# Experts' matmul operands at another distance in SBUF, a pad tile dropped, and casts placed later

## The chip, the cores and the metric

One core of a Trainium2 chip. The metric is the device time of one execution in microseconds (us); the time shown is the median of three runs.

## The reference, cut to what matters

```python
X = rfft(x, axis=1)                      # x: 8 sequences of 2496 rows, 256 columns
Yr = shrink(Xr @ w_r - Xi @ w_i + b_r)   # soft threshold, lam = 0.01
Yi = shrink(Xr @ w_i + Xi @ w_r + b_i)
x = irfft(Yr + 1j * Yi, n=2496, axis=1).reshape(19968, 256)
logits = x @ w_gate + modality_bias[modality_id]
e_idx = argmax(logits); gate_w = softmax(logits)[e_idx]
for e in range(8):                       # each row goes to one expert
    h = maximum(x[mask] @ w1[e], 0.0)    # 256 -> 1024
    out[mask] = gate_w[mask, None] * (h @ w2[e])   # 1024 -> 256
```

## The kernel before

The first part (up to 596 us in the profile) makes the Fourier transforms, the mixing and the routing: every row gets a place in a sorted array `xs` in DRAM, with 256 more rows of room behind each expert's own. The second part, class `Experts` (L801 on), works through that array.

`Experts.run` (L1233) goes through 38 tiles of 512 rows and 2 of 256, one expert per tile, and five small tiles of at most 32 rows in between (`tiny`, L1166), which fill single steps of TensorE's order. A tile's weights stand in one of two sets of SBUF tiles, `wb[i % 2]`; a set is `w0`, `w1` (layer 1, columns split in two groups) and `w2`, `w3` (layer 2, rows split likewise). Set 0 lies in the pool `mw0` on the right side of SBUF, at the end of memory; set 1 lies in `mw1` on the left side, behind the other pools of the part.

All experts' matmuls are fp32r, 128 rows by 256 columns, with every value split into a high and a low part, so a product of two blocks is three matmuls (high by high, high by low, low by high):

- Layer 1 (`layer1`, L1008, matmuls at L1024): the moving operand is the rows, `xh{j}` and `xl{j}` of pool `mxs`; the stationary one a block of `w0` or `w1`. From tile 8 on the 2x2 block product is done with seven products instead of eight, from sums of weights (made once, `weight_sums`) and of rows (`sums`): 7 products of 6 matmuls for each column group, 84 for a tile. Tiles 0 to 7 take 8 products for each group, 96.
- ScalarE and VectorE make `hh` and `hl` (pools `mh0`, `mh1`) of layer 1's result.
- Layer 2 (`layer2`, L1082, matmuls at L1095): here `hh`, `hl` are the stationary operand and `w2`, `w3` the moving one; 16 groups of 6 matmuls, 96 for a tile.

TensorE's order is written out by hand. A tile has two phases, `grp` 0 and 1. In phase 0 of tile i layer 1 of its own second column group goes with layer 2 of its first one (weights `w1`, `w2` of set i % 2); in phase 1 layer 1 of tile i + 1, first group (`w0` of the other set), goes with layer 2 of tile i, second group (`w3` of set i % 2). The string of `order` says which comes at each of 15 steps: "121212121221212", where a 1 is one product of layer 1 (6 matmuls) and a 2 is 6 matmuls of layer 2.

Beside it, tables say at which step a piece of other work is issued: `FILL[0]` (L1219) for phase 0, `FILL[1]` for phase 1. "x" is one turn of `parts(i + 1)` (L938): ScalarE casts one block of the next tile's rows to `xh{j}` (L958) and GpSimd subtracts to `xl{j}` (L959), j in the order 0, 1, 3, 2, 4, 5, 6. Each `xh{j}` has one buffer, so the cast of the next tile waits until layer 1's product on the old block is done. Blocks 2 to 5 are the row sums, made in place in the tile `xt`. "o", "t" and "p" are the output, the sums and the transposes.

`setup_pads` (L612) fills a tile with zeros and a number out of range; `pads` (L618) and `fence` (L640) write it behind each expert's rows with DMAs of SyncE's queue. The generator `late` (L1584) routes the last sequence, then calls `pads` and `fence`; it moves on at seven steps of each phase (`LATE`).

The pools lie one behind the other in SBUF in the order of `pools` (L811): `mx`, `mtr`, `mc`, a filler `mq0`, `mxs`, `ms`, a hidden-layer pair `mh0` and `mh1`, a filler `mq1`, `mw1`, `mb`. Fillers are sized by `PADS` (L46) in columns of 4 bytes. Sizes in bytes per partition: an `xh` or `xl` tile 1024, `ms` three tiles of 2048, `hh` and `hl` 8192 each, `w0` and `w1` 14336, `w2` and `w3` 8192. All of these are multiples of 512, and so is every block that a matmul takes of them; what an operand's start is modulo 512 is therefore set by the fillers and by the tiles of `mc` alone.

```python
PADS = (56, 16)                                                             # L46
pad = lambda name, n: n and pool(name, 1).tile([128, n], F32, name=name + "t")
for u in range(2):                                                          # L1021
    for k, (lo, x) in enumerate(((0, xh), (0, xl), (1, xh))):
        nc.tensor.matmul(ps[:, u, :], w1[:, lo, u, blk, :], x, ...)         # stationary, moving
...
nc.tensor.matmul(ps, h[:, q, o], w2[:, lo, q, :], ...)                      # L1095
```

Of the kernel before, what the change touches and what calls it, by code (L numbers as in the profile page):

```python
# [9 lines left out]
F32 = mybir.dt.float32  # L10
F32R = mybir.dt.float32r
# [12 lines left out]
D = 256  # L24
# [7 lines left out]
GC = D + E  # L32
# [10 lines left out]
MORE = 16  # L43
NPL = 8
EARLY = (6 * SEQ - 8 * (TP - 1)) // TP + 1 - E
PADS = (56, 16)  # L46
W1 = 2 * 2 * 4 * 128
W2 = 2 * 4 * 256
RAW = (2, 4, 6, 8, 10)
# [107 lines left out]
class Attn:  # L157
# [5 lines left out]
    def pools(self, ctx, first):  # L163
        tc, nb = self.tc, self.nb
        pool = lambda name, bufs, **k: ctx.enter_context(tc.tile_pool(name=name, bufs=bufs, **k))

        self.w6, self.w3, self.wx = (first.enter_context(tc.tile_pool(name=name, bufs=bufs, side="right"))
                                     for name, bufs in (("w6", 5), ("w3", 4), ("wx", 4)))
        self.ww = pool("ww", 2)
        self.wo = {"wh": pool("wh", 2), "wl": pool("wl", 2)}  # L170
        self.cp = pool("consts", 1)
        self.w4 = pool("w4", 4)
        self.wX = pool("wX", 3)
        self.w2 = pool("w2", 2)
        self.w1 = pool("w1", 1)
        self.cl = pool("cl", 1)
        self.ps = pool("ps", 2, space=PSUM)
        self.dr = pool("dr", 3, space=DRAM)
        self.scr = [None] * nb
        self.xt, self.xs, self.parts = {}, {}, []  # L180
# [616 lines left out]
class Experts:  # L797
# [8 lines left out]

    def sets(self, ctx, i, **k):
        p = ctx.enter_context(self.tc.tile_pool(name=f"mw{i}", bufs=1, reuse_waits="tile", **k))
        return [p.tile([128, 2, 2, 7, 128] if n < 2 else [128, 2, 4, D], F32R, name=f"w{n}_{i}") for n in range(4)]

    def pools(self, ctx):  # L811
        nc, tc, rt = self.nc, self.tc, self.rt
        pool = lambda name, bufs, **k: ctx.enter_context(
            tc.tile_pool(name=name, bufs=bufs, reuse_waits="tile", **k))
        pad = lambda name, n: n and pool(name, 1).tile([128, n], F32, name=name + "t")
        self.x = pool("mx", 2)
        self.tr = pool("mtr", 1)
        self.cp = pool("mc", 1)
        self.ident = self.cp.tile([128, 128], F32, name="mident")
        nc.gpsimd.memset(self.ident, 0.0)  # L820
        nc.gpsimd.affine_select(out=self.ident, in_=self.ident, compare_op=ALU.not_equal, fill=1.0, base=0,
                                pattern=[[-1, 128]], channel_multiplier=1)
        pad("mq0", PADS[0])
        self.xp = pool("mxs", 1)
        self.s = pool("ms", 1)
        self.h = [pool("mh0", 1), pool("mh1", 1)]
        pad("mq1", PADS[1])
        self.wb.append(self.sets(ctx, 1))
        self.b = pool("mb", 2)
        room = rt.at.x1f[0]  # L830
        self.raw = (room[:, :2 * F].rearrange("p (c f) -> p c f", c=2),
                    room[:, 2 * F:2 * F + 8 * D].rearrange("p (c d) -> p c d", d=D))
        self.small, o = {}, 2 * F + 8 * D
        for nm, n in (("xt", GC), ("xc", 256), ("x", 256), ("hs", 256), ("h", 256), ("y", 256), ("ix", 1)):
            self.small[nm], o = room[:, o:o + n], o + n
        self.ps = pool("mps", 2, space=PSUM)
        self.hps = pool("mhps", 1, space=PSUM)
# [369 lines left out]
    def sort_half(self, i):  # L1207
# [9 lines left out]
    FILL1 = {0: "x", 1: "o", 4: "x", 7: "x", 13: "x"}  # L1217
    FILL2 = {0: "x", 1: "o", 3: "t", 4: "x", 6: "x", 9: "x", 10: "x", 14: "x", 15: "x"}
    FILL = (  # L1219
        {0: "x", 1: "o", 3: "t", 4: "x", 6: "xx", 8: "x", 11: "x", 13: "x"},  # L1220
        {1: "o", 3: "p", 5: "p"})
    LATE = (2, 3, 5, 7, 9, 10, 12)

# [9 lines left out]
    def run(self, late, *tail):  # L1233
# [4 lines left out]
        for i in range(NPL - 2, -1, -1):  # L1238
            t = self.tags[i + 1]
            self.tags[i] = [t[3]] + [j for j in range(7) if j not in t]  # L1240
        pieces = self.weight_sums()
        for i in range(2):
            self.load_x(i)
        self.rt.setup_pads(self.cp.tile([128, GC], F32, name="pad2"))
        self.rt.grid2 = self.rt.load_grid(self.cp, "c_grid2", 5 * E + 3)
        for n in range(4):
            self.load_w(1, n)
# [111 lines left out]
def build(tc, I, out, nb):  # L1359
    nc = tc.nc  # L1360
    with ExitStack() as outer:
# [3 lines left out]
        with ExitStack() as ctx:  # L1365
            at = Attn(tc, I, nb)
            rt = Route(outer, tc, I, at, nb)
            front = ExitStack()
            at.pools(ctx, front)
            ex = None  # L1370
# [42 lines left out]
            i = at.table_load("m", 0, nc.gpsimd)  # L1413
# [41 lines left out]
            for b in range(nb):  # L1455
                done = b == nb - 1
                for p in range(10):
                    i = 10 * b + p
# [50 lines left out]
                    if done and p == 8:  # L1509
                        front.close()  # L1510
                        assert not (sw.todo or sw.raw)
                        ex = Experts(outer, tc, I, out, rt, wsp, wss)
# [67 lines left out]
        with ExitStack() as ctx:  # L1580
            ctx.enter_context(tc.manual_schedule(engines={ET.PE, ET.Activation, ET.DVE, ET.Pool}))
            ex.pools(ctx)

            def late():  # L1584
                for state in chain(routing, rt.tiles_last(ex.cp)):
                    yield
                    if state == "pe":
                        for _ in range(3):
                            yield
                while rt.pending:  # L1590
                    rt.scatter(1)
                    yield
                    yield
                for _ in range(12):
                    yield
                rt.pads()
                for _ in range(8):
                    yield
                rt.fence()
                rt.late = True  # L1600


            ex.run(late(), *tail)
# [24 lines left out]
```

## Time and profile before

| | |
|---|---|
| median of 3 runs | 1458.16 us (1457.96 to 1460.24) |
| the profiled execution | 1462.81 us |
| its span, first to last instruction | 1460.9 us |
| TensorE busy | 98% |
| mean granted clock of TensorE | 0.992 |

An engine's busy time is the union of its instructions' spans. A matmul's record (some 279 ns) is longer than the distance to the next matmul's start (some 116 ns), because matmuls are pipelined; what a stream of matmuls takes is read from the starts.

### The profile page before, as it was taken

What the parts mean: (1) busy time and instruction counts of PE and PEld (TensorE: products, weight loads), DVE (VectorE), ACT (ScalarE), POOL (GpSimd) and SP (SyncE); (2) the same over time, 40 slices, a digit from 0 to 9 for tenths busy, and PEclk for the clock granted to TensorE, in tenths of its full rate; (3) what the DMA queues carried; (4) which work ended last, traced back from release to release, by engine and by line L of the source; (5) the groups of instructions that cost most, each with busy time, mean ns of one, the idle gap of its engine ahead of it and who ended that gap; (6) DMA issues with size and microseconds to landing.
All of it is one profiled execution on the core that took longest, in us unless ns stands there. A gap on an engine that the chain in (4) does not pass through costs nothing. (4 is left out here: it accounts for less than half of the span.)

```text
span 1460.9 us, 33883 instructions
## 1 busy us (share of the span) xinstructions
PE 1427.8 (98%) x12084; PEld 1366.1 (94%) x12084; DVE 900.3 (62%) x1721; ACT 782.0 (54%) x1675; POOL 793.0 (54%) x907
## 2 busy tenths in 40 slices
PE   8899999999999999999999999999999999999996
PEld 5889999998989999999999999999999999999995
DVE  4567575757575876667565665666566656665651
ACT  3465656565656454544445555555555555555542
POOL 2355767676767666366667543444344444444432
PEclk9999999999999999999999999999999999999998
DMA  8979686969696759687787288124122942682192
GB/s 265 264 236 297 212 284 214 298 215 299 200 297 182 224 180 290 198 248 249 240 277 245 70 291 268 38 59 115 32 60 58 338 126 59 203 261 59 44 355 80
DMA packets 245299, 289.82 MB, mean 198 GB/s; under 512 B 121232, under 2 KB 176267, under 8 KB 241925
## 3 DMA queue, kind: packets, MB, share of 16 engines
q1 hardware_dynamic: 225587, 244.64, 54.4%
q0 software_dynamic: 19408, 42.83, 9.3%
q8 instruction: 98, 1.61, 0.5%
q14 instruction: 76, 0.62, 0.1%
q10 hardware_dynamic: 130, 0.12, 0.0%
HBM read 322.80 MB, written 117.56 MB: 301 GB/s over the span
## 5 line engine op out<-in xcount | busy, mean ns | idle before, releaser
L1095 PE MATMUL y<-w,hh 128*128 128x256 f32 x2496 | 461.4, 279 | 0.0
L1095 PEld LDWEIGHTS y<-w,hh 128*128 128x128 f32 x2496 | 380.8, 189 | 3.7 <-issue 3.7
L1095 PE MATMUL y<-w,hl 128*128 128x256 f32 x1248 | 346.8, 278 | 1.1 <-DVE hl L1030 0.9
L1024 PE MATMUL X<-xh,w 128*128 128x256 f32 x1248 | 270.3, 281 | 0.0
L1128 POOL DMA_INDIRECT out<-o,ix x156 | 155.4, 996 | 182.4 <-ACT o L1112 145.7
L1095 PEld LDWEIGHTS y<-w,hl 128*128 128x128 f32 x1248 | 234.2, 188 | 1.7 <-DVE hl L1030 1.7
L1024 PEld LDWEIGHTS X<-xh,w 128*128 128x128 f32 x1248 | 212.6, 188 | 2.0 <-ACT hh L1029 1.6
L1024 PE MATMUL X<-xl,w 128*128 128x256 f32 x624 | 174.6, 280 | 0.6 <-POOL xl L959 0.6
L1030 DVE SCALAR_TENSOR_TENSOR hl<-Y,hh 128x512 fp32r<-128x512 f32 x140 | 96.8, 692 | 102.9 <-ACT hh L1029 102.8
L1029 ACT ACTIVATE hh<-Y 128x512 fp32r<-128x512 f32 x140 | 83.8, 599 | 119.0 <-DVE Y L1033 101.1
L959 POOL TENSOR_TENSOR xl<-tr,xh 128x256 fp32r<-128x256 f32 x94 | 70.4, 749 | 129.2 <-ACT xh L958 128.7
L1024 PE MATMUL Z<-xh,w 128*128 128x256 f32 x608 | 131.8, 281 | 0.7 <-DVE Y L1033 0.7
L382 PE MATMUL mx<-wmix,Xh 128*128 128x256 f32 x640 | 116.6, 305 | 7.5 <-DVE mx L372 7.2
L959 POOL TENSOR_TENSOR xl<-xt,xh 128x256 fp32r<-128x256 f32 x122 | 89.5, 746 | 58.5 <-ACT xh L958 57.2
L1024 PEld LDWEIGHTS X<-xl,w 128*128 128x128 f32 x624 | 117.1, 188 | 1.0 <-POOL xl L959 0.8
L1038 ACT COPY v<-X 128x512 f32<-128x512 f32 x180 | 105.6, 587 | 17.5 <-PE X L1024 10.3
L598 POOL DMA_INDIRECT xs<-x1b,si x88 | 90.0, 1023 | 41.5 <-DVE pl L430 19.6
L424 PE MATMUL pv<-pv,z 128*120 128x136 f32 x704 | 108.5, 279 | 1.0 <-ACT z L414 0.9
L598 POOL DMA_INDIRECT xs<-x,si x88 | 89.5, 1017 | 36.0 <-issue 16.7
L292 POOL TENSOR_TENSOR x1l<-x,x1h 117x512 fp32r<-117x512 f32 x59 | 75.6, 1284 | 60.8 <-ACT x1h L290 21.9
L382 PEld LDWEIGHTS mx<-wmix,Xh 128*128 128x128 f32 x640 | 92.4, 190 | 16.4 <-ACT x1h L290 3.6
L1024 PEld LDWEIGHTS Z<-xh,w 128*128 128x128 f32 x608 | 103.7, 188 | 0.9 <-DVE Y L1033 0.9
(261 smaller groups left out, 3435.8 us busy)
## 6 DMA issues: line engine op xcount, KB each, us to landing
w<-wsp SPq DMA_DIRECT2D x96, 1024.0 KB
w<-wss SPq DMA_DIRECT2D x64, 1024.0 KB
w<-wsp SPq DMA_DIRECT2D x64, 768.0 KB
a<-scr SPq DMA_DIRECT2D x160, 128.0 KB
x<-in_x SPq DMA_DIRECT2D x38, 512.0 KB
xt<-xs SPq DMA_DIRECT2D x152, 128.0 KB
scr<-ev SPq DMA_DIRECT2D x35, 480.0 KB
wsp<-wh SPq DMA_DIRECT2D x64, 256.0 KB
```

Source lines behind the costliest of these rows:

```text
L292: (nc.gpsimd if pool else nc.vector).tensor_sub(xl, x, xh)
L382: nc.tensor.matmul(mx[:, i, :], t[:, c, 1 - i, :], self.w[:, i, c, lo, :], start=False, stop=n == 5, skip_group_check=True)
L424: nc.tensor.matmul(ps[:PK, c * 128:c * 128 + D // 2 + E], self.z[:, o:o + 3, :, :].rearrange("p n k r -> p (n k r)"), self.pv[:, c, :], st ...
L598: i = self.nc.gpsimd.indirect_dma_start(out=self.xs, out_offset=bass.IndirectOffsetOnAxis(ap=si[:, k:k + 1], axis=0), in_=rows, in_offset= ...
L959: (nc.gpsimd if i or j in (0, 1, 6) else nc.vector).tensor_sub(sq(xl), v, sq(xh))
L1024: nc.tensor.matmul(ps[:, u, :], w1[:, lo, u, blk, :], x, start=start and u == k == 0, stop=k == 2, skip_group_check=True)
L1029: nc.scalar.activation(hh[:, par::2, o], v, AF.Relu)
L1030: nc.vector.scalar_tensor_tensor(hl[:, par::2, o], v, 0.0, hh[:, par::2, o], ALU.max, ALU.subtract)
L1038: nc.scalar.copy(v, ps)
L1095: nc.tensor.matmul(ps, h[:, q, o], w2[:, lo, q, :], start=grp == s % 2 == q == k == 0, stop=grp == 1 and q == 3 and k == 2, skip_group_che ...
L1128: ins = self.nc.gpsimd.indirect_dma_start(out=self.out, out_offset=bass.IndirectOffsetOnAxis(ap=ix, axis=0), in_=o, in_offset=None, bounds ...
```

## The change

It does four things.

1. **Addresses.** A filler of 16 columns (64 bytes) stands between `ms` and `mh0`, one of 112 columns (448 bytes) in front of `mw1`, and each weight set now holds `w2`, `w3`, 16 columns of filler, then `w0`, `w1`.
2. **The pad tile.** `pad2` (264 columns, 1056 bytes) is no longer in `mc`; the pad rows are filled into the small tile's buffer `small["xt"]`, a piece of the first part's tile `x1`.
3. **When the pad rows are filled.** `setup_pads` is called one turn of `late` ahead of `pads`, no longer at the start of the part.
4. **Casts.** `FILL[0]` has its third to seventh "x" at steps 7, 8, 10, 12 and 14 instead of 6, 6, 8, 11 and 13. `FILL1` and `FILL2`, which tiles 0 to 7 use, stay.

```diff
--- before.py
+++ after.py
@@ -43,7 +43,7 @@
 MORE = 16
 NPL = 8
 EARLY = (6 * SEQ - 8 * (TP - 1)) // TP + 1 - E
-PADS = (56, 16)
+PADS = (56, 16, 112)
 W1 = 2 * 2 * 4 * 128
 W2 = 2 * 4 * 256
 RAW = (2, 4, 6, 8, 10)
@@ -806,7 +806,9 @@
 
     def sets(self, ctx, i, **k):
         p = ctx.enter_context(self.tc.tile_pool(name=f"mw{i}", bufs=1, reuse_waits="tile", **k))
-        return [p.tile([128, 2, 2, 7, 128] if n < 2 else [128, 2, 4, D], F32R, name=f"w{n}_{i}") for n in range(4)]
+        w2 = [p.tile([128, 2, 4, D], F32R, name=f"w{n}_{i}") for n in (2, 3)]
+        p.tile([128, 16], F32, name=f"mq2_{i}")
+        return [p.tile([128, 2, 2, 7, 128], F32R, name=f"w{n}_{i}") for n in (0, 1)] + w2
 
     def pools(self, ctx):
         nc, tc, rt = self.nc, self.tc, self.rt
@@ -823,8 +825,9 @@
         pad("mq0", PADS[0])
         self.xp = pool("mxs", 1)
         self.s = pool("ms", 1)
+        pad("mq1", PADS[1])
         self.h = [pool("mh0", 1), pool("mh1", 1)]
-        pad("mq1", PADS[1])
+        pad("mq3", PADS[2])
         self.wb.append(self.sets(ctx, 1))
         self.b = pool("mb", 2)
         room = rt.at.x1f[0]
@@ -1217,7 +1220,7 @@
     FILL1 = {0: "x", 1: "o", 4: "x", 7: "x", 13: "x"}
     FILL2 = {0: "x", 1: "o", 3: "t", 4: "x", 6: "x", 9: "x", 10: "x", 14: "x", 15: "x"}
     FILL = (
-        {0: "x", 1: "o", 3: "t", 4: "x", 6: "xx", 8: "x", 11: "x", 13: "x"},
+        {0: "x", 1: "o", 3: "t", 4: "x", 7: "x", 8: "x", 10: "x", 12: "x", 14: "x"},
         {1: "o", 3: "p", 5: "p"})
     LATE = (2, 3, 5, 7, 9, 10, 12)
 
@@ -1241,7 +1244,6 @@
         pieces = self.weight_sums()
         for i in range(2):
             self.load_x(i)
-        self.rt.setup_pads(self.cp.tile([128, GC], F32, name="pad2"))
         self.rt.grid2 = self.rt.load_grid(self.cp, "c_grid2", 5 * E + 3)
         for n in range(4):
             self.load_w(1, n)
@@ -1591,8 +1593,10 @@
                     rt.scatter(1)
                     yield
                     yield
-                for _ in range(12):
+                for _ in range(11):
                     yield
+                rt.setup_pads(ex.small["xt"])
+                yield
                 rt.pads()
                 for _ in range(8):
                     yield
```

Start addresses of the operands in the built programs, bytes modulo 512 (all blocks of one kind share the value):

| operand | before | changed |
|---|---|---|
| `xh`, `xl` (moving, layer 1) | 416 | 384 |
| `hh`, `hl` (stationary, layer 2) | 416 | 448 |
| `w0`, `w1` of set 1 (stationary, layer 1) | 480 | 448 |
| `w0`, `w1` of set 0 | 480 | 480 |
| `w2`, `w3` of set 1 (moving, layer 2) | 480 | 384 |
| `w2`, `w3` of set 0 | 480 | 416 |

The left side's values follow from the sizes: the 1056 bytes of `pad2` are 2 x 512 + 32, so `xh` moves from 416 to 384. Set 0 hangs on the end of memory and doesn't move along.

Where the order of instructions changes, on ScalarE, in phase 0 of tile 11 (any tile from 8 on reads alike; `xh{j}_12` is block j of the next tile, `v2`, `v3` are layer 1's copies out of PSUM, `hh1_11` the hidden layer). Before:

```order
L1038 COPY v2_11_1_12149<-X_11_1_12093 128x512
L958 CAST xh1_12_12151<-tr_12_11946 128x256
L958 CAST xh3_12_12168<-xt_12_11739 128x256
L958 CAST xh2_12_12172<-xt_12_11739 128x256
L1038 COPY v3_11_1_12188<-X_11_1_12093 128x512
L1029 ACTIVATE hh1_11_12091<-Y_11_1_12094 128x2x256
L958 CAST xh4_12_12193<-xt_12_11739 128x256
L1029 ACTIVATE hh1_11_12091<-X_11_1_12093 128x2x256
L958 CAST xh5_12_12218<-xt_12_11739 128x256
L1029 ACTIVATE hh1_11_12091<-Z_11_1_12095 128x2x256
L958 CAST xh6_12_12237<-tr_12_11946 128x256
```

With the change:

```order
L1041 COPY v2_11_1_12154<-X_11_1_12098 128x512
L961 CAST xh1_12_12156<-tr_12_11951 128x256
L961 CAST xh3_12_12179<-xt_12_11742 128x256
L1041 COPY v3_11_1_12189<-X_11_1_12098 128x512
L1032 ACTIVATE hh1_11_12096<-Y_11_1_12099 128x2x256
L961 CAST xh2_12_12194<-xt_12_11742 128x256
L961 CAST xh4_12_12211<-xt_12_11742 128x256
L1032 ACTIVATE hh1_11_12096<-X_11_1_12098 128x2x256
L961 CAST xh5_12_12229<-xt_12_11742 128x256
L1032 ACTIVATE hh1_11_12096<-Z_11_1_12100 128x2x256
L961 CAST xh6_12_12248<-tr_12_11951 128x256
```

The cast of `xh2` has moved behind the copy `v3` and the activation of `Y`; the others stand behind the same instructions as before.

On GpSimd, where the experts' part begins (`mident` is an identity matrix, the DMAs are the routing's). Before:

```order
L820 MEMSET mident_8216 128x128
L821 AFFINE_SELECT mident_8216<-mident_8216 128x128
L614 MEMSET pad2_8277 128x264
L598 DMA xs_68<-x1b_112,si_6_0_7592 162304x264 x2
L615 MEMSET pad2_8277 128x1
```

With the change:

```order
L822 MEMSET mident_8217 128x128
L823 AFFINE_SELECT mident_8217<-mident_8217 128x128
L598 DMA xs_68<-x1b_112,si_6_0_7592 162304x264 x2
L916 CAST ix_0_8300<-g_0_8267 128x4
L513 TENSOR_TENSOR b0_7_7990<-omid_7_7988,mb_515 117x176
```

The two fills of `pad2` are gone from here.

On GpSimd again, between phases 0 and 1 of tile 11 (`xl6_11` is the last subtraction of the next tile's rows). Before:

```order
L959 TENSOR_TENSOR xl4_11_11856<-xt_11_11421,xh4_11_11855 128x256
L959 TENSOR_TENSOR xl5_11_11881<-xt_11_11421,xh5_11_11880 128x256
L959 TENSOR_TENSOR xl6_11_11900<-tr_11_11640,xh6_11_11899 128x256
L1128 DMA out_0<-o_10_1_12009,ix_10_11415 19968x256 x2
L913 CAST ix_12_12070<-g_12_11740 128x4
```

With the change:

```order
L962 TENSOR_TENSOR xl5_11_11890<-xt_11_11424,xh5_11_11889 128x256
L962 TENSOR_TENSOR xl6_11_11909<-tr_11_11643,xh6_11_11908 128x256
L614 MEMSET x1_67 128x264
L615 MEMSET x1_67 128x1
L1131 DMA out_0<-o_10_1_12014,ix_10_11418 19968x256 x2
L916 CAST ix_12_12075<-g_12_11743 128x4
```

The two fills of the pad rows, now in a piece of `x1`, stand between the last subtraction and the output's DMAs. TensorE's and VectorE's orders are the same as before, and so is SyncE's apart from the tile that the pad DMAs read.

## Rows read from the trace of the kernel before

**Rows 1.** The page, head and part 1: busy us (share), instructions.

```profile
span 1460.9 us, 33883 instructions
...
PE 1427.8 (98%) x12084; PEld 1366.1 (94%) x12084; DVE 900.3 (62%) x1721; ACT 782.0 (54%) x1675; POOL 793.0 (54%) x907
```

**Rows 2.** Windows, layer 1's matmuls (L1024): stretch, us, PE, PEld, clock, DMA share, GB/s.

```profile
596.00:1450.00 854.00, 488.77 (x3384) 434.91 (x3384) 1.00 0.56 169
```

**Rows 3.** The same stretch, layer 2's matmuls (L1095).

```profile
596.00:1450.00 854.00, 527.62 (x3744) 475.79 (x3744) 1.00 0.56 169
```

**Rows 4.** Waits of TensorE, 596 to 1450 us: total us, times, longest.

```profile
PE y L1095 <- DVE hl L1030: 0.9, 1, 0.9
PE Z L1024 <- DVE Y L1033: 0.7, 1, 0.7
PE X L1024 <- POOL xl L959: 0.6, 1, 0.6
```

**Rows 5.** Timeline of TensorE, tile 12, groups' first matmuls: start us, us, ..., count merged.

```profile
855.03 0.28 PE L1024 MATMUL X<-xh,w 128*128 128x256 f32 x1
...
855.72 0.39 PE L1095 MATMUL y<-w,hh 128*128 128x256 f32 x2
...
856.40 0.28 PE L1024 MATMUL Y<-xh,w 128*128 128x256 f32 x1
...
857.11 0.40 PE L1095 MATMUL y<-w,hh 128*128 128x256 f32 x2
...
857.82 0.28 PE L1024 MATMUL X<-xh,w 128*128 128x256 f32 x1
...
858.51 0.39 PE L1095 MATMUL y<-w,hh 128*128 128x256 f32 x2
...
875.97 0.28 PE L1024 MATMUL X<-xh,w 128*128 128x256 f32 x1
```

**Rows 6.** The same timeline, tile 0, layer 1 alone: matmuls 6 and 49.

```profile
597.00 0.39 PE L1024 MATMUL X<-xh,w 128*128 128x256 f32 x2
...
601.87 0.28 PE L1024 MATMUL X<-xh,w 128*128 128x256 f32 x1
```

**Rows 7.** The same timeline, the last run of layer 2 alone, 16 matmuls.

```profile
1446.30 0.28 PE L1095 MATMUL y<-w,hl 128*128 128x256 f32 x1
...
1448.07 0.28 PE L1095 MATMUL y<-w,hl 128*128 128x256 f32 x1
```

**Rows 8.** The same timeline, layer 1 behind the transposes of a small tile.

```profile
1040.90 0.38 PE L1024 MATMUL X<-xh,w 128*128 128x256 f32 x1
...
1041.71 0.39 PE L1095 MATMUL y<-w,hh 128*128 128x256 f32 x2
...
1042.39 0.28 PE L1024 MATMUL Z<-xh,w 128*128 128x256 f32 x1
...
1440.87 0.36 PE L1024 MATMUL Y<-xh,w 128*128 128x256 f32 x1
...
1441.07 0.28 PE L1024 MATMUL Y<-xl,w 128*128 128x256 f32 x1
...
1442.37 0.28 PE L1024 MATMUL Y<-xh,w 128*128 128x256 f32 x1
```

**Rows 9.** Windows of all engines over one tile: us, PE, PEld, DVE, ACT, POOL, ...

```profile
1093.90:1114.80 20.90, 20.90 (x182) 20.90 (x181) 13.01 (x21) 11.72 (x25) 9.27 (x13) 1.00 0.24 51
```

**Rows 10.** Groups by line, 771 to 1416 us: casts and subtractions, busy us, mean ns.

```profile
L958 ACT CAST xh<-xt 128x256 fp32r<-128x256 f32 x118 | 45.0, 404 | 39.5 <-POOL xl L959 35.5 <-issue 4.0
...
L959 POOL TENSOR_TENSOR xl<-xt,xh 128x256 fp32r<-128x256 f32 x118 | 86.6, 745 | 58.5 <-ACT xh L958 57.2
```

**Rows 11.** Timeline of GpSimd: the fills of the pad rows, and around 838 us.

```profile
582.67 0.31 POOL L614 MEMSET pad<- 128x264 f32 x1
...
585.58 0.13 POOL L615 MEMSET pad<- 128x1 f32 x1
...
835.55 0.74 POOL L959 TENSOR_TENSOR xl<-tr,xh 128x256 fp32r<-128x256 f32 x1 [1.23 <-ACT xh L958]
...
840.63 1.00 POOL L1128 DMA_INDIRECT out<-o,ix  x1 [4.34 <-ACT o L1112]
```

## The prediction

> **What bounds the kernel now.** I read the page first: TensorE is busy 98% of a span of 1460.9 us [rows 1]. Then the windows of the experts' part: 3384 matmuls of layer 1 and 3744 of layer 2, 7128 together, in 854 us [rows 2, 3]. In that stretch TensorE waits for other engines 0.9 + 0.7 + 0.6 = 2.2 us in all [rows 4], and the granted clock is 1.00, the 2.4 GHz level. So the part lasts as long as its matmuls take from start to start, and only a change of that pace can move the time by much. The window over one tile shows the matmul and the weight load side by side without a gap: 20.90 us busy each, of 20.90 [rows 9].
>
> The timeline then shows that the pace isn't one number. From layer 1's first matmul of tile 12 at 855.03 to that of tile 13 at 875.97 are 180 matmuls in 20.94 us, **116.3 ns** each. But inside, two paces take turns [rows 5]: the group of 6 at 855.03 takes 0.69 us and the next one 0.68 (fast); those at 856.40 and 857.11 take 0.71 each (slow); the one at 857.82 takes 0.69 (fast again). The pace changes where layer 2 hands over to layer 1 (856.40, 857.82), not where layer 1 hands over to layer 2 (855.72, 857.11, 858.51). Away from handovers each pace holds: 43 matmuls of layer 1 alone at the part's start take 601.87 - 597.00 = 4.87 us, **113.3 ns** each [rows 6]; 15 matmuls of layer 2 alone at the end take 1.77 us, **118.0 ns** each [rows 7]. Same shape, same clock; what differs between the layers is where their operands lie. By the table of addresses layer 1's moving operand starts 64 bytes below its stationary one (416 and 480 modulo 512), layer 2's 64 bytes above. At a handover both ends swap, so the distance goes from one sign to the other.
>
> **The change, part by part.** The sum is made on the profiled execution, 1462.81 us, of which 1.9 lie outside the span; the median is 1458.16, 0.3% less, and I subtract the same microseconds from it.
>
> *Addresses.* They touch all 7128 matmuls and add none. With set 1 the moving operand now lies 64 bytes below the stationary one in both layers and at both handovers (384 and 448), the arrangement in which rows 6 run at 113.3 ns. With set 0 the end of memory fixes the weights, and the distances are 96 bytes (layer 1) and 32 (layer 2), of the same sign. Bounds come from the two paces: all fast gives 7128 x (116.3 - 113.3) ns = **21.4 us less**; all slow gives 7128 x (118.0 - 116.3) ns = **12.1 us more**. No row shows distances of 32 or 96 bytes; the nearest are those of 64, of either sign, so both bounds stand. I take the fast pace for 85% of the matmuls: 0.85 x 21.4 - 0.15 x 12.1 = 16.4 us less. The reasons: the only long undisturbed run with this sign is fast over 43 matmuls and seven changes of block; the handovers no longer turn the sign, and the steps that are left with set 0 are 32 bytes per operand instead of 64. The 15% are for the stretches behind small tiles, where the pace is drawn anew: behind the transposes of one small tile layer 2's six matmuls from 1041.71 to 1042.39 take 0.68 us (fast), behind those of another the 11 matmuls from 1441.07 to 1442.37 take 1.30 us, 118.2 ns each (slow) [rows 8].
>
> The matmul's two operand reads are where the Trainium skill speaks against this change. The rows show two paces for one shape, which switch at the same handover each time [rows 5]. "TensorE: Matmul & The Clock Gate", Part 2, step 1, says that TensorE has two independent read ports, so that loading the next weights takes no bandwidth from the running matmul; by that rule addresses can't set the pace and this part is worth 0. The trace doesn't bear it out as it stands, but it can't show either that the address is what sets the pace, so the case is a rival below.
>
> *Casts.* Per tile from 8 on the same seven casts of 0.40 us and subtractions of 0.75 us [rows 10] are issued, none more. The cast of `xh2` goes behind the copy `v3` and one activation, the others half a step later. What they feed is read by layer 1 of the next tile one phase, about 10 us, later, which hides the 1.15 us; without that cover it would be up to 1.15 us for each of some 30 tiles. ScalarE is busy 11.72 of 20.90 us [rows 9] and waits for GpSimd 35.5 us in 645 us ahead of casts of row sums [rows 10]; the copy `v3` comes 0.40 us sooner, but TensorE hardly waits for any of this, so the gain is bounded by the 2.2 us of rows 4, and I take 0. If TensorE gets 2.6% faster a tile lasts some 20.4 us, still far more than the 13.01 us of the busiest other engine [rows 9].
>
> *Pad rows.* Two fills, 0.31 + 0.13 us, leave GpSimd at 582.67 and 585.58 [rows 11]; the experts' steady stream of matmuls starts over 10 us later, at 597 [rows 6], so 0 (at most 0.4 us less). They come back between the subtraction that ends at 836.29 and the output's DMA at 840.63, a gap of 4.34 us in which GpSimd waits [rows 11]: 0 again. SyncE's pad DMAs wait for the fill, and the next tile's loads queue behind them; were the fill late, at most its 0.44 us would reach that queue. The tile that is filled was read by the routing's scatters, and the generator goes on for eleven turns, about one and a half phases of 10 us, between the last of them and the fill.
>
> Sum: 16.4 us from the median's 1458.16 gives **1441.8 us**.
>
> **The rivals.**
> 1. *The slow pace stays (slower).* The swap of sign throws the pace from fast to slow, but also from slow to fast: layer 2's slow run ends at 857.82 only because layer 1 takes over there [rows 5]. With one sign that way out is gone. If the breaks behind small tiles leave TensorE slow, as at 1441.07 [rows 8], it stays slow until the next small tile, six tiles on (`every` in `run`). Price: up to 12.1 us, 1470.3. It decides once more than 1 - 12.1 / (21.4 + 12.1) = 64% of the matmuls run slow. For it: rows 7 hold 118.0 ns to the end, and rows 8 show a slow start with the good sign. Against it: rows 6, and that all of rows 7 is the other sign. Chance 0.18.
> 2. *Only the exact 64 bytes count.* Set 1 alone serves both layers in phase 0 of odd tiles, a quarter of the matmuls; the rest goes on alternating. 0.25 x 21.4 = 5.4 us less, 1452.8; with half of the rest won, some 1447. For it: every run that I have is at exactly 64 bytes. Against it: a step of 32 is the smaller disturbance. Chance 0.20.
> 3. *Addresses don't matter.* The two paces then come from the instruction order (which operand changes from one matmul to the next), which stays; the time is 1458.2, and the change does nothing that it says. For it: the pace turns at handovers whatever the length of the runs between them. Against it: both layers use the same pattern of six, and differ in their addresses. This is what the skill's rule gives, too. Chance 0.12.
>
> A new wait can come with any of these: a faster TensorE asks for weights, rows and casts some 0.5 us a tile sooner. It waits for no DMA now [rows 4]; I leave a microsecond or two for it, inside the range.
>
> **How the numbers follow.** The forecast (most of the part fast, 12 to 22 us less) has 0.50, the rivals 0.18, 0.20 and 0.12. A measurement of this kernel can tell about 0.2%, 2.9 us, from no change. Faster by more than that: the forecast and nearly all of rival 2, 0.68. Slower: nearly all of rival 1, 0.18. Within: 0.14. The range must leave out no more than 2 in 10: its low end is all fast with the waits of rows 4 gone, 1458.2 - 21.4 - 2.2 = 1434.6; its high end 1464 cuts off the worse half of rival 1. Gains and losses are both in it; the forecast's own range is 1435 to 1446.
>
> **What would show it.** Right: groups of 6 at 0.68 us on both sides of every handover, in odd tiles' phase 0 first of all, and a tile of 8 to 37 in 20.4 to 20.6 us instead of 20.94. With set 0 in play (phase 0 of even tiles) the pace should be the same; if 0.71 stands there, the 32 bytes matter (rival 2). If all groups show 0.71 from one small tile to the next, it is rival 1; if fast and slow still take turns at the same handovers, rival 3. Casts and pad rows are right if TensorE's waits stay near 2 us and the fills lie in GpSimd's gap. The prediction is wrong if the time is above 1455 us.

## The result, and the profile after

The changed kernel takes **1470.68 us** (median of 6 runs, 1470.2 to 1472.52); the kernel before, in 6 runs, 1459.93. The ratio is 1.0077, with a 95% interval of 1.0062 to 1.0092: slower by 10.75 us, where 16.4 less were forecast. The profiled execution took 1470.91 us.

The head and part 1 of its page, which answer to [rows 1]:

```profile
span 1469.1 us, 33885 instructions
...
PE 1436.8 (98%) x12084; PEld 1376.1 (94%) x12084; DVE 898.7 (61%) x1721; ACT 783.5 (53%) x1675; POOL 790.2 (54%) x907
```

TensorE is busy 98% as before, but 9.0 us longer, with the same 12084 matmuls. Windows over the experts' part, layer 1's matmuls (L1027) and then layer 2's (L1098), with the columns of [rows 2, 3]:

```profile
593.70:1457.00 863.30, 494.02 (x3384) 440.92 (x3384) 1.00 0.55 167
...
593.70:1457.00 863.30, 534.11 (x3744) 480.49 (x3744) 1.00 0.55 167
```

The counts are the same 3384 and 3744, the granted clock is 1.00, and the stretch is longer. Waits of TensorE in the experts' part (total us, times, longest), against [rows 4]:

```profile
PE X L1027 <- POOL xl L962: 0.6, 1, 0.6
PE y L1098 <- DVE hl L1033: 0.6, 1, 0.6
```

They are 1.2 us, not 2.2. So no wait has come in; the matmuls themselves stand further apart. The timeline of TensorE shows by how much. Each row below is the first matmul of a phase, and 90 expert matmuls lie between a row and the next:

```profile
856.49 0.28 PE L1027 MATMUL X<-xh,w 128*128 128x256 f32 x1
...
867.05 0.28 PE L1027 MATMUL X<-xh,w 128*128 128x256 f32 x1
...
877.75 0.28 PE L1027 MATMUL X<-xh,w 128*128 128x256 f32 x1
...
888.37 0.29 PE L1027 MATMUL X<-xh,w 128*128 128x256 f32 x1
...
898.98 0.28 PE L1027 MATMUL X<-xh,w 128*128 128x256 f32 x1
```

The four phases take 10.56, 10.70, 10.62 and 10.61 us, that is 117.3 to 118.9 ns a matmul; a tile takes 21.26 us (856.49 to 877.75) and 21.23 (877.75 to 898.98), where [rows 5] have 20.94. The phase from 888.37 to 898.98 is phase 0 of an odd tile, where only set 1 is used and all distances are 64 bytes. The groups of such a phase, two tiles later:

```profile
936.06 0.28 PE L1027 MATMUL Y<-xh,w 128*128 128x256 f32 x1
...
936.76 0.40 PE L1098 MATMUL y<-w,hh 128*128 128x256 f32 x2
...
937.47 0.28 PE L1027 MATMUL X<-xh,w 128*128 128x256 f32 x1
...
938.18 0.40 PE L1098 MATMUL y<-w,hh 128*128 128x256 f32 x2
```

The groups of six take 0.70, 0.71 and 0.71 us, on both sides of each handover. Here the paces no longer take turns: all is slow, 117.8 ns. In the phase from 856.49, layer 1 has set 0's 96 bytes and layer 2 set 1's 64, and the groups still differ, by layer:

```profile
857.89 0.28 PE L1027 MATMUL Y<-xh,w 128*128 128x256 f32 x1
...
858.61 0.40 PE L1098 MATMUL y<-w,hh 128*128 128x256 f32 x2
...
859.30 0.28 PE L1027 MATMUL X<-xh,w 128*128 128x256 f32 x1
```

From 857.89 to the phase's end layer 1 takes 120.4 ns a matmul and layer 2 114.9. In the whole part no more than nine distances in a row stay under 115 ns. At the part's start, layer 1 alone with set 0's 96 bytes, matmuls 6 and 49 of the part as in [rows 6]:

```profile
594.80 0.28 PE L1027 MATMUL X<-xh,w 128*128 128x256 f32 x1
...
599.85 0.28 PE L1027 MATMUL X<-xh,w 128*128 128x256 f32 x1
```

5.05 us for 43 matmuls, 117.4 ns, where [rows 6] have 4.87 us. Over the whole part I took the mean distance between the starts of neighbouring expert matmuls, leaving out the 65 or so of 160 ns and more (waits, other work in between, and the restarts behind either): 118.0 ns, before 116.3. This mean is "the pace" in all that follows, and a place that was left out is a "break".

The account: 7128 x (118.0 - 116.3) ns = 12.1 us more; the distances left out exceed 117 ns by 5.5 us in all, before by 6.8, so 1.3 less (those with other matmuls in them aside, which hold some 16.2 us either way). That makes 10.8, and the stretch from the start of the first expert matmul to that of the last did grow from 852.1 to 862.8 us, by 10.7. The two profiled executions differ by 8.1 us only: the part begins 2.2 us sooner in the one of after, and the one of before lay 2.9 us over its median.

Casts and subtractions, in groups by line over the stretch of [rows 10]:

```profile
L962 POOL TENSOR_TENSOR xl<-xt,xh 128x256 fp32r<-128x256 f32 x117 | 85.3, 749 | 65.3 <-ACT xh L961 65.1
...
L961 ACT CAST xh<-xt 128x256 fp32r<-128x256 f32 x117 | 44.7, 404 | 39.5 <-POOL xl L962 36.1 <-issue 3.3
```

The timeline of GpSimd where the pad rows are filled, with the columns of [rows 11]:

```profile
836.63 0.74 POOL L962 TENSOR_TENSOR xl<-tr,xh 128x256 fp32r<-128x256 f32 x1 [0.92 <-ACT xh L961]
...
837.30 0.32 POOL L614 MEMSET x<- 128x264 f32 x1
...
837.68 0.10 POOL L615 MEMSET x<- 128x1 f32 x1
...
841.87 1.00 POOL L1131 DMA_INDIRECT out<-o,ix  x1 [4.09 <-ACT o L1115]
```

The cast still takes 0.404 us and the subtraction 0.749, and the casts' idle time behind GpSimd is 36.1 us, not 35.5. The two fills of the pad rows stand at 837.30 and 837.68, inside a gap of the kind that [rows 11] show, ahead of the output's DMA.

### The profile page after: what moved, and what is told of

Same layout as the page of the kernel before. It is cut to its first block, busy times and chain, and to the rows that moved or that the text cites. A ratio compares the mean times of both kernels' runs of the same rounds, so it can differ in the third digit from the quotient of the medians.

```text
span 1469.1 us, 33885 instructions
## 1 busy us (share of the span) xinstructions
PE 1436.8 (98%) x12084; PEld 1376.1 (94%) x12084; DVE 898.7 (61%) x1721; ACT 783.5 (53%) x1675; POOL 790.2 (54%) x907
## 5 line engine op out<-in xcount | busy, mean ns | idle before, releaser
L1098 PE MATMUL y<-w,hh 128*128 128x256 f32 x2496 | 466.3, 281 | 0.0
L1098 PEld LDWEIGHTS y<-w,hh 128*128 128x128 f32 x2496 | 381.3, 188 | 3.7 <-issue 3.7
L1098 PE MATMUL y<-w,hl 128*128 128x256 f32 x1248 | 350.6, 281 | 0.7 <-DVE hl L1033 0.6
L1027 PE MATMUL X<-xh,w 128*128 128x256 f32 x1248 | 273.7, 282 | 0.0
L1098 PEld LDWEIGHTS y<-w,hl 128*128 128x128 f32 x1248 | 236.0, 189 | 1.3 <-DVE hl L1033 1.3
L1027 PEld LDWEIGHTS X<-xh,w 128*128 128x128 f32 x1248 | 214.5, 190 | 2.0 <-ACT hh L1032 1.6
L1027 PE MATMUL X<-xl,w 128*128 128x256 f32 x624 | 176.1, 282 | 0.6 <-POOL xl L962 0.6
L1027 PE MATMUL Z<-xh,w 128*128 128x256 f32 x608 | 133.0, 282 | 0.0
L1027 PEld LDWEIGHTS X<-xl,w 128*128 128x128 f32 x624 | 117.6, 188 | 1.1 <-POOL xl L962 0.8
L1027 PEld LDWEIGHTS Z<-xh,w 128*128 128x128 f32 x608 | 104.4, 190 | 0.0
```

Of the source, the lines that this page charges most:

```text
L1027: nc.tensor.matmul(ps[:, u, :], w1[:, lo, u, blk, :], x, start=start and u == k == 0, stop=k == 2, skip_group_check=True)
L1098: nc.tensor.matmul(ps, h[:, q, o], w2[:, lo, q, :], start=grp == s % 2 == q == k == 0, stop=grp == 1 and q == 3 and k == 2, skip_group_che ...
```

## The experiments

Fifteen kernels ran, all but e10 made from the changed one. In them `GAPS[i]` is the filler, in columns, between the two pairs of weight tiles of set i, in place of the 16 columns that `sets` has for both; `PADS` are the fillers ahead of the rows, the hidden layer and set 1. Columns: the distance from the moving to the stationary operand in bytes modulo 512 (the same in layer 1, layer 2 and both handovers unless said otherwise); the pace; the first to the last expert matmul; the time, and that of the kernel before in the same series. Two paces are given where a run holds stretches of each. The times of e1, e2, e9, e10 and e15 are medians of 10, 4, 6, 4 and 7 runs; the others ran once, so their times have no interval, and the argument rests on their paces.

| run | distance | pace, ns | experts' part, us | time, us | kernel before, us |
|---|---|---|---|---|---|
| e1 | as before | 116.3 | 854.2 | 1491.23 | 1490.91 |
| e2 | 64, at 416 and 480 | 113.6 | 836.7 | 1477.88 | 1490.91 |
| e3 | 448 (64 with the other sign) | 117.3 (113.3 and 117.8) | 860.8 | 1505.07 | 1490.91 |
| e4 | 0 | 120.0 | 879.0 | 1515.19 | 1490.91 |
| e5 | 64, at 384 and 448 | 114.7 (113.3 and 117.8) | 843.1 | 1484.27 | 1486.57 |
| e6 | 32 | 118.3 | 867.3 | 1501.16 | 1486.57 |
| e7 | 96 | 118.4 | 867.4 | 1504.86 | 1486.57 |
| e8 | 128 | 118.7 | 869.5 | 1503.53 | 1486.57 |
| e9 | 64, at 416 and 480 | 113.6 | 838.2 | 1442.85 | 1459.72 |
| e10 | the change | 118.0 | 862.6 | 1470.2 | 1459.72 |
| e11 | 256 | 120.0 | 875.8 | 1484.1 | 1459.72 |
| e12 | 192 | 117.8 (a few us at 113.3) | 861.5 | 1468.29 | 1459.72 |
| e13 | 64, layer 1 with set 0 96 | 115.9 (115.6 behind a break at 759 us) | 852.1 | 1487.4 | 1491.24 |
| e14 | 64, layer 2 with set 0 32 | 117.9 | 864.7 | 1505.06 | 1491.24 |
| e15 | 64, at 384 and 448 | 114.1 (113.3 and 117.8) | 841.3 | 1479.12 | 1491.24 |

The series ran on several chips, on some of which the kernel before takes 1487 to 1491 us. Most of that difference lies ahead of the experts' part, which began at 621.7 us in e1's profile and at 596.0 in the one of before; the pace is the same to 0.1 ns (e1 against before, e2 against e9, e10 against the change). So paces are compared across series, times only within one.

**e1: the change with the old starts.**

```diff
-PADS = (56, 16, 112)
+GAPS = (0, 0)
+PADS = (64, 0, 16)
...
-        p.tile([128, 16], F32, name=f"mq2_{i}")
-        return [p.tile([128, 2, 2, 7, 128], F32R, name=f"w{n}_{i}") for n in (0, 1)] + w2
+        w1 = [p.tile([128, 2, 2, 7, 128], F32R, name=f"w{n}_{i}") for n in (0, 1)]
+        GAPS[i] and p.tile([128, GAPS[i]], F32, name=f"mq2_{i}")
+        return w1 + [p.tile([128, 2, 4, D], F32R, name=f"w{n}_{i}") for n in (2, 3)]
```

> All of the change (pad tile dropped, pad rows filled late, casts later), but fillers that put every operand back on the starts of before, modulo 512: rows and hidden layer 416, all weights 480. Theory A (the starts alone make the loss): the time of before, about 1460 us, within 0.2%, and the two paces take turns again (groups of 6 at 0.68 and 0.71 us). Theory B (casts or pad rows make the loss): about 1470 us.

Ratio 0.9994 (0.9973 to 1.0016), pace 116.3 ns. Theory A: casts, pad tile and pad rows together are worth nothing that can be measured, and the starts make the whole loss.

**e2 and e9: 32 bytes more.**

```diff
-PADS = (56, 16, 112)
+GAPS = (16, 16)
+PADS = (64, 16, 112)
```

(e10 is the changed kernel itself, beside e9.)

> The change with one number more: the filler ahead of the rows is 64 columns instead of 56, so that the left side is 32 bytes further on and the moving operand lies exactly 64 bytes below the stationary one everywhere, with set 0 too (rows and second-layer weights 416, hidden layer and first-layer weights 480). Theory A1 (any one distance leaves the slow pace standing, since nothing throws it out): about 1470 us, 117.8 ns a matmul in all four kinds of phase. Theory A2 (the distances of 32 and 96 bytes with set 0 make the loss): 1440 to 1450 us, 113 to 115 ns in most phases.

> The kernel with the moving operand exactly 64 bytes below everywhere (416 and 480), again, for its time against the kernel before. 113.6 ns a matmul in place of 116.3 is 7128 x 2.7 ns = 19 us: ratio 0.987 if the first part keeps its time, 0.991 as in its first timing.

> The changed kernel itself, in the same series as the kernel with exactly 64 bytes. 118.0 ns a matmul, the experts' stretch 863 us; 1.0077 times the kernel before if the pace is all that counts.

One number turns the loss into a gain: 0.9906 (0.9882 to 0.993) in e2, **0.9883** (0.986 to 0.9906) in e9, beside which the change itself stood at 1.0079 (1.006 to 1.0098). Theory A2. The same timeline rows in e9, 90 matmuls apart:

```profile
858.97 0.28 PE L1028 MATMUL X<-xh,w 128*128 128x256 f32 x1
...
869.17 0.28 PE L1028 MATMUL X<-xh,w 128*128 128x256 f32 x1
```

10.20 us, 113.3 ns. But the pace is worth 7128 x 2.7 = 19 us, and the experts' part got only 852.1 - 838.2 = 13.9 us shorter. The rest is given back in waits and in the clock behind them. The two longest waits of TensorE in e9's experts' part:

```profile
PE y L1099 <- DVE hl L1034: 2.1, 2, 2.0
PE Z L1028 <- DVE Y L1037: 2.0, 1, 2.0
```

[Rows 4] have the same two at 0.9 and 0.7 us.

The timeline of VectorE at the one for `Y`:

```profile
898.65 1.30 DVE L914 STREAM_TRANSPOSE tr<-xt 128x512 f32<-128x512 f32 x2 [4.73 <-DMA xt<-xs]
899.88 0.67 DVE L1037 TENSOR_TENSOR Y<-Z,v 128x512 f32<-128x512 f32 x1
```

VectorE's transpose of the next rows waited for their load; the subtraction that makes `Y` stands behind it, and TensorE waited 2.0 us. Some 1.3 us into its work again the clock fell: a window of all engines over that stretch (us, PE, PEld, DVE, ACT, POOL, clock, DMA share, GB/s):

```profile
901.90:905.10 3.20, 3.20 (x18) 3.20 (x17) 1.90 (x4) 1.81 (x5) 0.24 (x1) 0.50 0.24 46
```

The granted clock is 0.50 there, the 1.2 GHz level. 16 matmuls stand 213 ns apart before it comes back, at a cost of 16 x 100 ns = 1.6 us. The same happened once more, behind the wait for `hl` at 721 us. The distances of 160 ns and more come to 12.2 us over 117 ns each, again without those that hold other matmuls, against 6.8 before: the 5.4 us that are missing.

**e3 and e4: the other sign, and none.**

e3 has the weight tiles in e1's order, `w0`, `w1`, filler, `w2`, `w3`:

```diff
-PADS = (56, 16, 112)
+GAPS = (16, 16)
+PADS = (80, 112, 0)
```

e4 has no filler but the first:

```diff
-PADS = (56, 16, 112)
+GAPS = (0, 0)
+PADS = (80, 0, 0)
```

> The same uniform distance with its sign reversed: the moving operand 64 bytes above the stationary one everywhere (480 and 416). Theory A1 (one distance, no turns, the slow pace stands): about 1470 us, 118 ns. Theory A3 (the sign decides, and I had it the wrong way round): about 1440 us, 113.5 ns.

> The same with distance 0 everywhere: all four kinds of operand start at 480 modulo 512. Theory A1 (one distance, the slow pace stands, whatever it is): about 1470 us, 118 ns. Theory A4 (the distance between the two reads sets the pace, and 64 bytes is a bad one): another time, anywhere from 1438 (113.3 ns) up; above 1475 us if reads that start alike are the worst case.

e4 is one pace, 120.0 ns, from end to end, and 24.3 us over the kernel before: A4 with its worst case, not A1. e3 is mostly A1, but not wholly: it ran at 113.3 ns for 84 us. The timeline where this began:

```profile
674.55 0.19 PE L659 MATMUL t_psb<-t_indb,tri 117*128 117x40 bf16 x1
...
674.80 0.28 PE L1028 MATMUL X<-xl,w 128*128 128x256 f32 x1
...
675.36 0.39 PE L1099 MATMUL y<-w,hh 128*128 128x256 f32 x2
...
676.04 0.28 PE L1028 MATMUL Y<-xh,w 128*128 128x256 f32 x1
...
676.72 0.39 PE L1099 MATMUL y<-w,hh 128*128 128x256 f32 x2
```

Behind one small matmul of other work (L659) layer 1 starts again, and the groups from 674.80 on take 0.56 (five matmuls), 0.68 and 0.68 us. The fast pace then held over all handovers until TensorE waited at 758.78; from there on it was 117.8. So this sign has both paces too, and A3 falls.

**e5 and e15: 64 bytes at other starts.**

```diff
+GAPS = (16, 16)
...
+        i or p.tile([128, 8], F32, name="mq4")
```

The last line stands behind `w0` and `w1` and adds 32 bytes there in set 0 alone; `PADS` are the change's.

> The change with 32 bytes of filler behind set 0 at the end of memory, so that set 0 comes to the starts of set 1: moving operands at 384, stationary ones at 448 everywhere, 64 bytes apart as in the run with 416 and 480, which took 113.6 ns a matmul. Theory C1 (only the distance counts; the change was slow with set 1 because set 0's 32 and 96 bytes threw TensorE into the slow pace and it stayed there): 113.6 ns, the experts' stretch 836 to 838 us. Theory C2 (the starts themselves count, 384 and 448 are worse than 416 and 480): 117.8 ns, as with set 1 in the change, some 866 us.

> The run with 64 bytes at 384 and 448 once more, in the same series. If the pace is drawn at each break and held until the next, its mean changes from run to run between 113.4 and 117.8 ns (114.7 in the first), all in stretches of either 113.3 or 117.8; the time lies between 1442 and 1470 us and its runs scatter more than those of a kernel with one pace.

This differs from the change by set 0's 32 bytes alone, and its pace is 114.7 and 114.1 ns, its ratio in e15 0.9925 (0.9898 to 0.9952). Not C2's 117.8 throughout; C1 in its mechanism, though its 113.6 was not reached. Both paces are there, each in long stretches: e5 ran slow to 759 us, fast to about 840, slow to 945, then almost wholly fast; e15 was slow from about 650 to 755, then almost wholly fast. The timeline of e5 at one such border:

```profile
757.70 0.28 PE L1030 MATMUL X<-xh,w 128*128 128x256 f32 x1
...
758.41 0.40 PE L1101 MATMUL y<-w,hh 128*128 128x256 f32 x2
...
759.46 0.39 PE L1101 MATMUL y<-w,hl 128*128 128x256 f32 x1 [0.30 <-DVE hl L1036]
759.68 0.28 PE L1030 MATMUL X<-xh,w 128*128 128x256 f32 x1
...
760.37 0.39 PE L1101 MATMUL y<-w,hh 128*128 128x256 f32 x2
...
761.05 0.28 PE L1030 MATMUL X<-xh,w 128*128 128x256 f32 x1
...
761.73 0.39 PE L1101 MATMUL y<-w,hh 128*128 128x256 f32 x2
```

The group at 757.70 takes 0.71 us, layer 2 waits for `hl`, and behind the wait the groups take 0.69, 0.68 and 0.68. So the pace is drawn at a break and held until the next one; handovers between operands of one distance don't touch it. In the six runs with one distance of 64, 192 or 448 it never changes away from a break, but for a few matmuls right behind one. The wider scatter that e15 was to show is missing: its seven runs span 6.5 us, the ten of the kernel before 13.0.

The draw is not free, though; it goes largely by the place in the program. Behind each of the four small tiles between 905 and 1345 us the five restarts come out slow, fast, slow, fast, fast in e2 and in e9, and fast, slow, slow, fast, fast in e5 and in e15, and each of the two kernels ran on two chips. So at one distance the starts (416 and 480, or 384 and 448) may still bear on which pace a restart takes; no run settles that.

**e6, e7, e8, e11, e12: other distances.**

In the order of these five runs:

```diff
-PADS = (56, 16, 112)
+GAPS = (8, 8)
+PADS = (72, 8, 120)
...
+GAPS = (24, 24)
+PADS = (56, 24, 104)
...
+GAPS = (32, 32)
+PADS = (48, 32, 96)
...
+GAPS = (64, 64)
+PADS = (16, 64, 64)
...
+GAPS = (48, 48)
+PADS = (32, 48, 80)
```

> Uniform distance 32 (moving 448, stationary 480 everywhere). Theory C1 with 32 as a bad distance: 117.5 to 119 ns, about 868 us for the experts' stretch. Theory C3 (any distance above zero is as good as 64, and only its alternation between the sets costs): 113.6 ns, 837 us.

> Uniform distance 96 (moving 384, stationary 480 everywhere). With moving operands at 384 this also bears on C2. Theory C1 with 96 as a bad distance: 117 to 120 ns (the change's layer 1 at 96 bytes took 120.0 in the mean). Theory C3: 113.6 ns.

> Uniform distance 128 (moving 352, stationary 480 everywhere). If the pace follows the distance in steps of 64 (0: 120.0, 64: 113.6), 128 is as good as 64 or back at 120; if it falls with the distance, under 113.6 ns. A period of 128 would give 120 ns, the same as distance 0.

> Uniform distance 256 (moving 224, stationary 480). 0 took 120.0 ns, 32 118.3, 64 113.6, 96 118.4, 128 118.7, 448 (the reversed 64) 117.3. If what counts is the distance modulo 256, 120 ns again; if 64 alone is good, 117 to 120; a second good distance would show 113.3 and lie near 19 us under the kernel before.

> Uniform distance 192 (moving 288, stationary 480). If odd multiples of 64 have a fast pace to be in (64 has, 448 kept it in a few stretches), 192 shows 113.3 ns in at least some stretches between two breaks and 117 to 118 in the others; if 64 alone has one, 117 to 120 throughout.

32 and 96 hold no stretch at 113.3 ns: their distances between matmuls run from 115 to 123 ns, and the mean is 118.3 and 118.4. C3 falls. 96 has two paces of its own, 117.3 and 118.7 ns, each held from break to break. 256 repeats 0 at 120.0 ns; 128 is at 118.7, neither of the values expected. 192 ran at 117.8 with a few us at 113.3, the two values of 64 and 448. So three odd multiples of 64 show the same pair of paces, and no other distance tried does. All but 64 ran at one pair of starts, so that the distance alone counts is shown for 64 and argued for the rest.

**e13 and e14: which half of set 0.** Both differ from e5, which has everything at 64 bytes, in one pair of set 0's weight tiles by 32 bytes.

e13 against the change (`w2`, `w3` of set 0 go down by 32 bytes to 384, `w0`, `w1` stay at 480):

```diff
+GAPS = (24, 16)
```

e14 against e5 (`w2`, `w3` of set 0 go up by 32 bytes to 416):

```diff
-GAPS = (16, 16)
+GAPS = (8, 16)
```

> The run with 64 bytes at 384 and 448 (114.7 ns), but set 0's first-layer weights 32 bytes further on: distance 96 for layer 1 with set 0, 64 everywhere else. It has the first half of what the change does with set 0. Theory D1 (each of the two distances is enough to throw TensorE out of the fast pace, and the phases at 64 bytes carry the slow pace on): 117.5 to 118.5 ns, set 1's phases at 117.8. Theory D2 (only layer 2's 32 bytes do it): 114 to 115.5 ns.

> The other half: set 0's second-layer weights 32 bytes further on, distance 32 for layer 2 with set 0, 64 everywhere else. Theory D1: 117.5 to 118.5 ns, set 1's phases at 117.8. Theory D3 (only layer 1's 96 bytes do it): 114 to 115.5 ns.

The phases' first matmuls in e13's timeline, 90 matmuls apart. The phases from 883.71 and 894.29 have layer 1 with set 0, at 96 bytes; those from 873.51 and 904.86 have nothing but 64:

```profile
873.51 0.28 PE L1028 MATMUL X<-xh,w 128*128 128x256 f32 x1
...
883.71 0.28 PE L1028 MATMUL X<-xh,w 128*128 128x256 f32 x1
...
894.29 0.28 PE L1028 MATMUL X<-xh,w 128*128 128x256 f32 x1
...
904.86 0.28 PE L1028 MATMUL X<-xh,w 128*128 128x256 f32 x1
...
915.05 0.28 PE L1028 MATMUL X<-xh,w 128*128 128x256 f32 x1
```

The same in e14. The phases from 901.05 and 911.70 have layer 2 with set 0, at 32 bytes; those from 922.35 and 932.95 have nothing but 64:

```profile
901.05 0.28 PE L1030 MATMUL X<-xh,w 128*128 128x256 f32 x1
...
911.70 0.28 PE L1030 MATMUL X<-xh,w 128*128 128x256 f32 x1
...
922.35 0.28 PE L1030 MATMUL X<-xh,w 128*128 128x256 f32 x1
...
932.95 0.28 PE L1030 MATMUL X<-xh,w 128*128 128x256 f32 x1
...
943.54 0.28 PE L1030 MATMUL X<-xh,w 128*128 128x256 f32 x1
```

e13: 10.20, 10.58, 10.57 and 10.19 us. The phases with 96 bytes are slower, and behind them the fast pace (113.3 ns) comes back, with no break in between. e14: 10.65, 10.65, **10.60** and **10.59** us. The last two are at 117.8 ns, although nothing in them lies at any other distance than 64. How e14 loses the fast pace can be read off. It ran fast from a break at 764.6 us on; tile 6 begins at 768.89, and the group at 769.57 is the first of layer 2 with set 0:

```profile
764.81 0.28 PE L1030 MATMUL Y<-xh,w 128*128 128x256 f32 x1
...
768.89 0.28 PE L1030 MATMUL X<-xh,w 128*128 128x256 f32 x1
...
769.57 0.40 PE L1101 MATMUL y<-w,hh 128*128 128x256 f32 x2
...
770.27 0.28 PE L1030 MATMUL X<-xh,w 128*128 128x256 f32 x1
...
770.98 0.40 PE L1101 MATMUL y<-w,hh 128*128 128x256 f32 x2
```

36 matmuls take 4.08 us (113.3 ns) and the group at 768.89 0.68; the one at 769.57 takes 0.70 and the next 0.71. No break lies there. So it is D2 in its mechanism: layer 2's 32 bytes throw TensorE out of the fast pace at once, and the phases at 64 bytes behind them stay slow. D2's number for e13 (114 to 115.5) was too low for two reasons: up to a break at 759 us e13 held the slow pace in all its phases (117.8), and behind it 96 bytes cost some 120 ns in layer 1's own matmuls; the mean from there on is 115.6, of the whole 115.9.

## Why the prediction was wrong

*The bound.* Right. TensorE's pace sets the time, and the whole difference lies in it; the account above closes to 0.1 us.

*The term of the addresses.* Its two bounds were right: all slow was to cost 12.1 us, and the loss is 10.75. That the starts set the pace was right as well: e1 shows that they alone make the loss, and e2 and e9 that one distance of 64 bytes runs fast. That e9's 1442.85 us lie so near the 1441.8 forecast is partly luck: its pace is worth more than was forecast, 19 us, and 5.4 of them are lost behind waits. The step that failed is "I take the fast pace for 85% of the matmuls", and of its reasons this one: "the steps that are left with set 0 are 32 bytes per operand instead of 64". It treated 32 bytes as a smaller disturbance. 32 and 96 are no smaller steps away from 64 but distances that have no fast pace (e6, e7), and one of them, layer 2's 32, leaves TensorE slow in phases that are themselves at 64 (e14). In the change these phases run at 117.8 ns, the whole part at 118.0; never are more than nine distances in a row under 115 ns, where 85% of the matmuls were to be fast.

*The sign.* "The arrangement in which rows 6 run at 113.3 ns" took the sign for the cause. e3 ran 84 us at 113.3 ns with the other sign, and e5 started its part at 117.8 ns with this one. What [rows 6, 7] show is which of two paces was drawn, not which sign is good. That the pace holds across handovers where the distance doesn't change is what the runs bear out. Why before it turned at the handovers from layer 2 to layer 1 and not at the others, where the sign changes too, no run shows.

*Rival 1.* Its time was right (1470.3), and its sign, 0.71 us in every group, nearly so (0.72 and 0.69 in the phase from 856.49). Its reason was only half right. The slow pace does stay (e5 held it for 88 and 101 us), but the breaks behind small tiles are not what leaves the change slow: e14 shows set 0's layer 2 throwing it back with no break.

*Rival 2.* Half right too: only distances like 64 count. But it let set 1's quarter run fast and the rest go on alternating, for 5.4 us less. (With half of the rest won its own terms give 5.4 + 8.0 = 13.4 us less, 1444.8, not 1447.) It overlooked that the phases with set 1 take over the pace of the phases ahead of them.

*Rival 3.* Fell with e1 against e2: the same experts' instructions in the same order, 116.3 and 113.6 ns. The rule of the Trainium skill that the prediction weighed ("TensorE: Matmul & The Clock Gate", Part 2, step 1) is that loading the next weights takes no bandwidth from the running matmul. Read as the prediction read it, that addresses can't set the pace, it doesn't hold here: e4's 120.0 and e9's 113.3 ns, both at a granted clock of 1.00, differ by addresses alone, and the measurement decides. Whether the two reads get in each other's way, or what else does it, no run shows.

*Casts and pad rows.* 0 stands: e1 bounds the three together at -0.27% to +0.16%, 4.0 us less to 2.4 more, and its pace is the one of before. The fills lie in the gap of GpSimd that was named.

*The new wait.* "I leave a microsecond or two" was too little for a fast pace: e9 lost 5.4 us, since a row load and the clock behind the wait came into it.

What stays open: what in a restart draws the fast pace or the slow one. I counted the restarts that took 198 to 232 ns and had 16 expert matmuls behind them. In e2, e5, e9 and e15 (64 bytes) 75 of 97 that took 219 to 223 ns led into the fast pace, but 12 of 32 that took 200 to 205; in e3 and e12 (448 and 192) 2 of 62 in all. So 64 is the best of the three by its restarts, not by its paces, and no run tells why the place in the program decides as it does. Open too: why layer 2's 32 bytes spoil the next phases and layer 1's 96 don't; and why the experts' part begins 2.2 us sooner with the change (593.77 against 595.96 us; 592.3 to 593.9 in e9 to e12).

## What to carry to other kernels

Where a stream of matmuls alternates weight loads and reads, vary the start of one operand against the other and read the pace from the starts of the matmuls: here it moved from 113.3 to 120.0 ns at the same clock, for nothing but fillers. Such a distance must hold for every pair that meets, in each buffer set; here one set 32 bytes off cost the whole gain and some 11 us more. (Smaller steps, and the handovers by themselves, were not tried.) And a good stretch in a trace shows that a state exists, not what causes it: look for the same arrangement in the other state before building on it.

## What the runs showed that I had not expected

- The pace of 128 x 256 matmuls in fp32r, each with its own weight load, by the distance of the two operands' starts modulo 512: 120.0 ns at 0 and 256, 118.7 at 128, 118.3 at 32, 118.4 at 96 (the mean of 117.3 and 118.7), and 113.3 or 117.8 at 64, 192 and 448. Most of these are one run each.
- At these last three the pace is a state: it is drawn at a break and held over hundreds of matmuls (88 us and more), through all changes of layer and block, until the next break or until a pair at another distance comes in (e14). e5 and e15 are one kernel, and their slow stretches differ in part (e15 starts fast and lacks the one from 843 to 945 us), but behind the four small tiles they draw alike.
- In e9 each of two waits of 2.0 us was followed, some 1.3 us into the work behind it, by the 1.2 GHz level (granted clock 0.50) for 16 matmuls, 213 ns apart, 1.6 us on top of the wait.
